# Two transformer layers on one core: the first weight group, GpSimd's copies, the first transpose and the last copies are arranged anew

## The chip, the core and the metric

The kernel runs on one core of a Trainium2 chip. The core has five engines, each with its own queue of instructions that it takes in order: TensorE (PE: matrix products, which write to PSUM), VectorE (DVE), ScalarE (ACT), GpSimd (POOL) and SyncE (SP, which here issues DMA transfers). Semaphores order the engines among each other. SBUF is the working memory, PSUM holds matmul results in 8 banks. The metric is the device time of one execution in microseconds; the profile is of a single execution of its own.

## The reference

```python
def _A_ref(x, wqkv, wo):                 # H = 32 heads of 16, S = 2048, D = 512
    qkv = (x @ wqkv).reshape(B, S, 3, H, Dh)...
    scores = einsum("bhqd,bhkd->bhqk", q, k) * Dh ** -0.5
    o = einsum("bhqk,bhkd->bhqd", softmax(scores), v)
    return o... @ wo
def _B_ref(x, w1, w2):                   # Dff = 1792
    return relu(x @ w1) @ w2
for both layers:
    x = x + _A_ref(layernorm(x), wqkv, wo)
    x = x + _B_ref(layernorm(x), w1, w2)
```

All inputs are bf16; both layers use the same weights.

## The kernel before, in words

**The stream of exps.** Each of the two layers has 32 heads x 2048 x 2048 scores. They are made in slots: in a slot TensorE writes three banks of 128 x 512 scores (`ps_s0` or `ps_s1`, in turn; line 1692), and ScalarE takes the exponential of them in one instruction (line 1705) into one of five buffers `e`. In most slots ScalarE takes only two banks (1024 columns); the third is read by VectorE, which makes an approximate exponential of three such banks by integer arithmetic (`lin`, line 1278; `up` and `down`, line 1330). The weighted sums with V go to `ps_o` (line 1158, "PV"): a round is up to four matmuls of 32 columns of weights side by side, one for each of four head pairs, and starts 0.216 us after the one before. K, Q and V projections, the output projection and the two feed-forward products are groups of such rounds (line 539) that fill TensorE's time between the scores; VectorE takes their results out of `ps_f` or `ps_o`.

**The plan.** What TensorE and VectorE do between the scores is decided while the program is built: a planner holds times of its own for TensorE (`now_pe`), VectorE (`now_dve`), the exps (`exp_end`), the SP queue (`sp_free`) and GpSimd (`pool_free`), and puts into each slot what it takes to be ready. `fill_v(limit, least)` places PV rounds if at least so many of the four head pairs have a block ready. When TensorE is too idle over the plan's window of 3.4 us, the same scores are written again (`times`). Constants tell the plan when x rows (`X_AT`), weight groups (`WQ_AT`) and V's weights (`WV_AT`) are there. `sp_lag` adds each issue on SP to `sp_free`. The engines run the resulting lists in order, with semaphores; a wait that the plan did not foresee blocks what stands behind it.

**The head.** x rows and weights are loaded by DMAs from SP, ScalarE and GpSimd queues. The columns of `wqkv` for K and Q are loaded in four groups T of 128 columns, K (k=0) and Q (k=1) each, and put in another order by one copy for each (`interleave`, line 205: `stage` to `wkq`). Group 0 of K is copied by ScalarE after its first two `xnT` copies, group 0 of Q by VectorE after the fourth normalized row; GpSimd copies the other three groups, as the DMAs land. Four rows of 128 tokens are normalized (statistics at line 575, root on GpSimd at line 1387, `head_apply` at line 1404), transposed on TensorE (line 635) and copied to `xnT` (line 1416; the first two by ScalarE, the last two by VectorE), with matmuls in between that only keep TensorE busy (line 1356). Then come the first K and Q projections (line 1422), Q's scaling (line 1455) and the first slot. Later chunks of 512 tokens are normalized by VectorE (line 626) and transposed by DMAs that SP issues (line 675).

**The tail.** After the last slot the last 128 rows are finished in line: output projection, normalization, transposition into one bank of `ps_o`, two half copies to `xnT` (line 1860: VectorE, then ScalarE), first feed-forward product in 14 steps with relu by VectorE and ScalarE in turn (lines 1885 and 1883), second product into one bank of 512 columns (line 1776), and two half copies of 256 columns out of that bank (line 1899: ScalarE, VectorE), each followed by its DMA to the output (line 1900).

Of the kernel before, what the change touches and what calls it, by code (L numbers as in the profile page):

```python
# [12 lines left out]
BF16 = mybir.dt.bfloat16  # L13
# [12 lines left out]
def kernel(  # L26
# [60 lines left out]
    BOTH = 4  # L87
    WHOLE = 4
    STARTS, MORE, ORDER = {}, {}, {}
    X_AT = (9.9, 10.1, 11.0, 11.4, 11.6, 11.9, 12.2, 12.5, 13.5, 14.5, 15.0, 15.5)  # L90
    WQ_AT, WV_AT = {0: 0.0, 1: 12500.0, 2: 16500.0, 3: 17900.0}, 9900.0
    VLAG = 1
    RSTD_LAG = 4000.0
    Q_SPARE = 6
# [21 lines left out]
    def sb(shape, dt, name):  # L116
        return persist.tile(shape, dt, name=name)
# [62 lines left out]
    ta2 = sb([P, 2, TPC], FP32, "ta")  # L180
    ta_ = [ta2[:, n] for n in range(2)]
    warm = sb([P, 1], FP32, "warm")

    ps_s = [psum.tile([P, W, QS], FP32, name=f"ps_s{n}") for n in range(2)]
    ps_o = psum.tile([P, QS], FP32, name="ps_o")
# [17 lines left out]
    def interleave(copy, k, T):  # L203

        copy(
            out=wkq[:, k, T].rearrange("p c (g d e) -> p (c g) e d", g=4, e=2),
            in_=stage[:, k, T].rearrange("p c (g e d) -> p (c g) e d", g=4, e=2),
        )
# [84 lines left out]
        made[key] = (engine, (now_pe if engine == "pe" else now_dve)[0] + lag)  # L293

    sp_free = [0.0]
    pool_free = [0.0]
    spread_till = [0.0]

# [350 lines left out]
    def ln_rows(tag, tt, n, i):  # L649

        if tag not in ln_seq:
            ln_seq.append(tag)
        at_tag = ln_seq.index(tag)
        prev = ln_seq[at_tag - 1]
        rows_of_prev = chunks[prev[1:]][1]
        before_that = ln_seq[at_tag - 2] if at_tag > 1 else None
        old = each(chunks[before_that[1:]][1], "xn", before_that) if at_tag > 1 else []
        if ("st", tag, i) not in made:
            loaded = [("x", tt + i)] * (tag[0] == "ln1" and not tag[1])
            task(720, lambda: ln_stats(tag, tt + i, i), [("st", tag, i)], old + loaded)  # L660
        if i == n - 1:

            def rstd():
                ln_seed(tag, n)
                pool_free[0] = max(pool_free[0], now_dve[0]) + RSTD_LAG
                mark(("rs", tag, 3), lag=pool_free[0] - now_dve[0])

            task(0, rstd, [("rs", tag, 3)], each(n, "st", tag) + old)
            def apply(k):
                ln_apply(tag, tt + k, k)  # L670
                if not by_dma(tag):
                    return
                _, l, j = tag
                xn_waits[0] -= k == TPC - 1
                nc.sync.dma_start_transpose(
                    out=xnT[j][:, :, k * P : (k + 1) * P], in_=xnbuf[k][:]
                )
                lag = sp_lag(TRANSPOSE) + (CROWDED if now_dve[0] < LOADED else 0.0)
                mark(("xT", tag, k), lag=lag)
                mark(("xnT", tag, k), lag=lag)  # L680
                if k == TPC - 1:
                    xn_free[0] = now_dve[0] + lag

            for k in range(n):
                task(
                    325, lambda k=k: apply(k),
                    [("xn", tag, k)] + [("xT", tag, k), ("xnT", tag, k)] * by_dma(tag),
                    [("xT", prev, k)] * (k < rows_of_prev) + [("rs", tag, 3)]
                    + [("raw",)] * (k == TPC - 1 and ("raw",) in made),
                )  # L690
# [700 lines left out]
        if not n:  # L1391
            set_ones(11, 16)
    for k in range(2):
        interleave(nc.gpsimd.tensor_copy, 1 - k, 1)
    set_ones(16, len(ones))
    for T in range(2, 4):
        for k in range(2):
            interleave(nc.gpsimd.tensor_copy, k, T)

    def head_bank(n, w):  # L1400
        return ps_s[n][:, w, :] if n < 2 else ps_f[:]

# [36 lines left out]
    for n in range(2):  # L1439
        for i in range(n * HALF, (n + 1) * HALF):  # L1440
            head_apply(i)
        if n:
            interleave(nc.vector.tensor_copy, 1, 0)
        for i in range(n * HALF, (n + 1) * HALF):
            head_transpose(i)
        if not n:
            interleave(nc.scalar.copy, 0, 0)
        idle_matmuls((4, 3)[n])
    head_k(0, P, (2, 0))
    for i in range(TPC):  # L1450
        head_q(i)
# [68 lines left out]
    pace = 0.0  # L1520
    recents = [[], []]
    readers = [[], []]
    now_pe[0] = 10900.0
    now_dve[0] = 12400.0
    exp_end = {-1: 10400.0, 0: 11400.0}
    pool_free[0] = WQ_AT[3]
    sp_free[0] = 15500.0
    pair_at = None
# [11 lines left out]
    while units:  # L1540
# [128 lines left out]
        for kind in ("v", "f", "v") if late else ("f", "v", "f"):  # L1669
            if kind == "f":  # L1670
                fill_pe(limit)
            else:
                fill_v(limit, 3 if len(pend) > 2 else 4)

        spare = int(max(need_by - pe_start("s", s_ready), 0.0) / MM)
        soon = (len(pend) > 1) + (owed[0] > 1.0 and (bool(cur) or not evac and any(
# [177 lines left out]
    while evac:  # L1854
        do_evac()
    for i in rows:
        pt = ln_transpose(tag, i, at_bank(more[i]).bitcast(BF16), more[i])
        for n, copy in enumerate((nc.vector.tensor_copy, nc.scalar.copy)):
            cs = slice(n * NDC // 2, (n + 1) * NDC // 2)
            uses(copy(out=xnT[NQS - 1][:, cs, part(i)], in_=pt[:, cs]), more[i], "xnT")  # L1860
    run_all()
    assert not w1_to_load
    ending[0], wide[0] = False, True
# [1 line left out]

    while half_done[0] < NF:
        half_part()
    for i in rows:
        add(banks[i], ident[:], x_t[tt + i][:], True, False, "x")
    for ft in range(NF + LOOK):  # L1870
        if ft == NF // 2:
            for b, x, row in outs:
                uses(nc.scalar.copy(out=x, in_=at_bank(b)), b)
                nc.sync.dma_start(out=out_flat[row * P : (row + 1) * P, :], in_=x)
        if ft < NF:
            b = more[ft % 4]
            for c in range(NDC):
                add(
                    b, w1_last[ft][:, c, :], xnT[NQS - 1][:, c, at_column : at_column + width],
                    c == 0, c == NDC - 1, "xnT",  # L1880
                )
            if ft % 2:
                out = nc.scalar.activation(out=ht[ft][:, at_column : at_column + width], in_=at_bank(b)[:, 0:width], func=ACTF.Relu)
            else:
                out = nc.vector.tensor_scalar(
                    out=ht[ft][:, at_column : at_column + width], in0=at_bank(b)[:, 0:width],
                    scalar1=0.0, scalar2=None, op0=ALU.max,
                )
            uses(out, b, "h")
        if ft >= LOOK:  # L1890
            for i in rows:
                add(
                    banks[i], ht[ft - LOOK][:, part(i)], w2[:, ft - LOOK, :],
                    False, ft == NF + LOOK - 1, "h",
                )
    for i in rows:
        for copy, queue, a in ((nc.scalar.copy, nc.scalar, 0), (nc.vector.tensor_copy, nc.sync, D // 2)):
            cols = slice(a, a + D // 2)
            uses(copy(out=x_t[tt + i][:, cols], in_=at_bank(banks[i])[:, cols]), banks[i])
            queue.dma_start(  # L1900
                out=out_flat[(tt + i) * P : (tt + i + 1) * P, cols], in_=x_t[tt + i][:, cols]
            )


# [28 lines left out]
```

## Time and profile before

| | |
|---|---|
| median of 3 runs | 1451.44 us (1450.73 to 1453.77) |
| the profiled execution | 1455.52 us; span of its instructions 1453.8 us |
| busy: ScalarE, TensorE, VectorE, GpSimd | 1424.2, 1366.6, 1312.1, 97.6 us |
| exps of 1536, 1024 and 512 columns | 369, 996 and 1 (1518, 1094 and 678 ns each) |
| first exp starts, last exp starts | 13.75 us, 1436.92 us |
| mean granted TensorE clock | 0.999 |

The span runs from the first to the last instruction of the profiled execution. Durations of successive exps overlap by some 0.19 us: starts of exps that are not held up lie 1.331 us apart behind one of 1536 columns and 0.904 us behind one of 1024. In lines of the timeline the first two numbers are start and length in microseconds; in brackets stands how long the engine was idle before, and what ended that. In lines of the windows each engine has its busy time and count, then come the granted TensorE clock, the DMA share and GB/s.

### The profile page before, as it was taken

Reading aid. Unit: us, or ns where it says so; the run is one execution under the profiler, and the core shown is the slowest. Engines: PE = TensorE matmul, PEld = TensorE weight load, DVE = VectorE, ACT = ScalarE, POOL = GpSimd, SP = SyncE. Lnnn points to the kernel's source line nnn. Section 1 sums busy time; section 2 is a strip of 40 time slices with the busy share of each in tenths; the row PEclk is TensorE's granted clock in tenths of the full one; section 3 lists DMA queues with packets and bytes.
Section 4 is the critical chain, followed back from the end, with each engine's and each line's share of the span. In section 5 each row is a group of like instructions: output and inputs, shape, how many; then the busy total and the mean of one; then the engine's idle time right before and its main releaser. Section 6 shows DMA issues by size and latency. Waiting matters only on the chain.

```text
span 1453.8 us, 47075 instructions
## 1 busy us (share of the span) xinstructions
PE 1366.6 (94%) x20730; PEld 507.1 (35%) x20732; DVE 1312.1 (90%) x2421; ACT 1424.2 (98%) x1385; POOL 97.6 (7%) x248
## 2 busy tenths in 40 slices
PE   8899999999999999999899999889999999999998
PEld 3222223222222222322323223222234444545665
DVE  7979999999999899999599889899989689999954
ACT  6999999999999999999999999999999999999996
POOL 5000001001010011000000000001001001010000
PEclk9999999999999999999999999999999999999999
DMA  5301100211012010110101000000110210313020
GB/s 142 84 6 25 23 11 16 44 27 31 10 26 48 19 22 10 39 42 17 24 5 37 24 5 2 10 15 13 44 41 20 50 36 23 74 35 80 13 59 19
DMA packets 135182, 46.23 MB, mean 32 GB/s; under 512 B 119968, under 2 KB 132192, under 8 KB 134976
## 3 DMA queue, kind: packets, MB, share of 16 engines
q1 hardware_dynamic: 127920, 37.08, 10.8%
q0 software_dynamic: 5568, 5.15, 1.9%
q8 instruction: 162, 2.65, 0.7%
q10 hardware_dynamic: 1488, 0.98, 0.2%
q14 instruction: 44, 0.36, 0.1%
HBM read 24.38 MB, written 2.10 MB: 18 GB/s over the span
## 4 chain that ended last, share of the span: by engine, by line
ACT 67%; PE 22%; DVE 9%; issue 1%; DMA 1%; POOL 0%; DVEq 0%; ACTq 0%
ACT e L1705 67%; PE ps_s L1692 7%; PE ps_f L539 7%; PE ps_o L1158 6%; DVE lin L1278 3%; DVE up L1330 1%; DVE down L1330 1%; PE ps_s L1776 1%; DVE ht L864 1%; PE ps_f L532 1%; DVE stats L575 0%; DVE q L787 0%; DVE vaug L771 0%; DVE x L904 0%; DVE ht L1025 0%
## 5 line engine op out<-in xcount | busy, mean ns | idle before, releaser
L1705 ACT ACTIVATE e<-ps_s 128x1024 bf16<-128x1024 f32 (+1 forms) x1366 | 1416.2, 1209 | 7.9 <-PE ps_s L1692 5.6
L1278 DVE TENSOR_SCALAR lin<-ps_s 128x512 int16<-128x512 f32 x996 | 664.1, 683 | 30.1 <-PE ps_s L1692 24.6
L1692 PE MATMUL ps_s<-q,ktp 32*128 32x512 bf16 (+2 forms) x6208 | 576.6, 324 | 48.3 <-ACT e L1705 42.7
L1158 PE MATMUL ps_o<-e,vaug 128*32 128x512 bf16 (+2 forms) x4318 | 395.8, 326 | 6.5 <-DVE r L1050 1.3
L1692 PEld LDWEIGHTS <-ktp 32*128 32x128 bf16 x6208 | 180.1, 91 | 520.3 <-issue 504.0
L1158 PEld LDWEIGHTS <-vaug 128*32 128x32 bf16 x7135 | 176.0, 95 | 225.9 <-issue 196.5
L1330 DVE TENSOR_SCALAR up<-lin 128x1536 int16<-128x1536 int16 x332 | 182.5, 550 | 12.0 <-PE ps_o L1158 11.2
L1330 DVE TENSOR_SCALAR down<-lin 128x1536 int16<-128x1536 int16 x332 | 182.0, 548 | 2.5 <-PE ps_o L1158 2.5
L1158 PE MATMUL ps_o<-up,vaug 128*32 128x512 bf16 (+2 forms) x1314 | 171.3, 329 | 0.0
L1158 PE MATMUL ps_o<-lin,vaug 128*32 128x512 bf16 (+2 forms) x1314 | 159.9, 329 | 1.3 <-DVE ht L1023 0.6
L1158 PE MATMUL ps_o<-down,vscaled 128*32 128x512 bf16 (+2 forms) x1125 | 148.7, 333 | 0.0
L539 PE MATMUL ps_f<-w,ht 128*32 128x512 bf16 x1680 | 130.7, 382 | 1.5 <-DVE ht L864 0.9
L539 PE MATMUL ps_f<-xnT,w 128*32 128x512 bf16 (+1 forms) x1792 | 123.7, 355 | 6.2 <-DVE ht L864 3.8
L539 PE MATMUL ps_f<-xnT,wkq 128*32 128x512 bf16 (+2 forms) x1376 | 102.5, 354 | 8.0 <-DMA xnT<-xn 2.3
L864 DVE TENSOR_SCALAR ht<-ps_f 128x512 bf16<-128x512 f32 (+1 forms) x111 | 74.2, 668 | 23.5 <-PE ps_f L539 16.6
L539 PEld LDWEIGHTS <-w 128*32 128x32 bf16 x1792 | 41.7, 95 | 43.0 <-issue 31.7
L1158 PEld LDWEIGHTS <-vscaled 128*32 128x32 bf16 x1125 | 49.7, 96 | 18.6 <-issue 10.6
L539 PEld LDWEIGHTS <-ht 128*32 128x32 bf16 x1680 | 35.9, 95 | 39.3 <-issue 27.0
L539 PEld LDWEIGHTS <-wkq 128*32 128x32 bf16 x1376 | 33.2, 95 | 39.1 <-issue 30.5
L539 PE MATMUL ps_f<-wv,xnT 128*32 128x512 bf16 x480 | 38.9, 387 | 6.9 <-DVE vaug L771 3.8
L575 DVE BATCH_NORM_STATS2 stats<-x 128x6 f32<-128x512 bf16 x63 | 42.3, 682 | 1.5 <-DMA x<-in_A_x_dram 1.2
L539 PE MATMUL ps_f<-wo,ot 128*32 128x512 bf16 x496 | 41.4, 382 | 0.7 <-DVE x L825 0.5
(138 smaller groups left out, 552.0 us busy)
## 6 DMA issues: line engine op xcount, KB each, us to landing
w<-in_B_w_dram SPq DMA_DIRECT2D x144, 128.0 KB
q<-xn SPq DMA_DIRECT2D x42, 64.0 KB
out_dram<-x SPq DMA_DIRECT2D x15, 128.0 KB
x<-in_A_x_dram SPq DMA_DIRECT2D x14, 128.0 KB
u<-r POOLq DMA_DIRECT2D x12, 128.0 KB, 4.7
ktp<-in_B_w_dram SPq DMA_DIRECT2D x10, 128.0 KB
u<-ht POOLq DMA_DIRECT2D x6, 128.0 KB, 4.4
r<-r SPq DMA_DIRECT2D x6, 128.0 KB
```

Source lines behind the costliest of these rows:

```text
L532: nc.tensor.matmul(out, lhsT, rhs, start=i % k == 0, stop=i % k == k - 1, skip_group_check=True,)
L539: nc.tensor.matmul(out[cols], lhsT[:, cols], rhs, start=i % k == 0, stop=i % k == k - 1, tile_position=(0, 32 * g), skip_group_check=True,)
L575: nc.vector.bn_stats(out=stats[ln_n(tag)][:, i, :], in_=x_t[tt][:])
L864: nc.vector.tensor_scalar(out=out, in0=sums, scalar1=0.0, scalar2=None, op0=ALU.max)
L1158: nc.tensor.matmul(ps_o[32 * g : 32 * g + 32, 0 : sg["w"]], values[:, 4 * sg["T"] + g, 2 * e : 2 * e + 32], rhs, start=g not in sg["begun" ...
L1278: first = nc.vector.tensor_scalar(out=lin[which][:, half * QS : (half + 1) * QS], in0=src, scalar1=EXP_BIAS, scalar2=0.0, op0=ALU.add, op1 ...
L1330: nc.vector.tensor_scalar(out=out, in0=line, scalar1=by, scalar2=0.0, op0=ALU.add, op1=ALU.max)
L1692: score = nc.tensor.matmul(b[:, a : a + sg["w"]], kt[32 * g : 32 * g + 32, kc : kc + P], qbuf[sg["n"] % 2][32 * g : 32 * g + 32, sg["e"], ...
L1705: ex = nc.scalar.activation(out=eb[:, 0 : place[m]], in_=b[:, 0 : place[m]], func=ACTF.Exp, scale=1.0 / (LOG2E * UNIT),)
L1776: uses(nc.tensor.matmul(out, lhsT, rhs, start=first, stop=last), b, needs=needs)
```

## The change

ScalarE makes both copies of group 0 (K and Q), before its two `xnT` copies; VectorE has no such copy any more. GpSimd first copies one column of the fourth normalized row into a new tile `after`, which makes it wait for that row, and then does its six weight copies and a dozen memsets, in the order T = 1, memsets, T = 2, T = 3. The plan counts 1.6 us more on SP behind the first DMA transpose, has other times for x, the weights and the start of the stream, and PV rounds are placed with three ready head pairs of four whatever is pending. In the tail the transposed last rows go into two banks, one for each half copy, and the last product into two banks of 256 columns, one for each of the last copies; the number of its matmuls doubles, with half the columns each.

```diff
--- before.py
+++ after.py
@@ -87,8 +87,9 @@
     BOTH = 4
     WHOLE = 4
     STARTS, MORE, ORDER = {}, {}, {}
-    X_AT = (9.9, 10.1, 11.0, 11.4, 11.6, 11.9, 12.2, 12.5, 13.5, 14.5, 15.0, 15.5)
-    WQ_AT, WV_AT = {0: 0.0, 1: 12500.0, 2: 16500.0, 3: 17900.0}, 9900.0
+    X_AT = (8.3, 8.5, 9.5, 10.6, 11.0, 11.4, 11.8, 12.1, 12.5, 12.8, 13.3, 14.0)
+    WQ_AT, WV_AT = {0: 0.0, 1: 10600.0, 2: 16000.0, 3: 17400.0}, 10200.0
+    FIRST_TRANSPOSE = 1600.0
     VLAG = 1
     RSTD_LAG = 4000.0
     Q_SPARE = 6
@@ -180,6 +181,7 @@
     ta2 = sb([P, 2, TPC], FP32, "ta")
     ta_ = [ta2[:, n] for n in range(2)]
     warm = sb([P, 1], FP32, "warm")
+    after = sb([P, 1], BF16, "after")
 
     ps_s = [psum.tile([P, W, QS], FP32, name=f"ps_s{n}") for n in range(2)]
     ps_o = psum.tile([P, QS], FP32, name="ps_o")
@@ -293,6 +295,7 @@
         made[key] = (engine, (now_pe if engine == "pe" else now_dve)[0] + lag)
 
     sp_free = [0.0]
+    first_transpose = [FIRST_TRANSPOSE]
     pool_free = [0.0]
     spread_till = [0.0]
 
@@ -675,6 +678,8 @@
                 nc.sync.dma_start_transpose(
                     out=xnT[j][:, :, k * P : (k + 1) * P], in_=xnbuf[k][:]
                 )
+                sp_free[0] = max(sp_free[0], now_dve[0] + 200.0) + first_transpose[0]
+                first_transpose[0] = 0.0
                 lag = sp_lag(TRANSPOSE) + (CROWDED if now_dve[0] < LOADED else 0.0)
                 mark(("xT", tag, k), lag=lag)
                 mark(("xnT", tag, k), lag=lag)
@@ -1391,12 +1396,7 @@
         if not n:
             set_ones(11, 16)
     for k in range(2):
-        interleave(nc.gpsimd.tensor_copy, 1 - k, 1)
-    set_ones(16, len(ones))
-    for T in range(2, 4):
-        for k in range(2):
-            interleave(nc.gpsimd.tensor_copy, k, T)
-
+        interleave(nc.scalar.copy, k, 0)
     def head_bank(n, w):
         return ps_s[n][:, w, :] if n < 2 else ps_f[:]
 
@@ -1439,13 +1439,15 @@
     for n in range(2):
         for i in range(n * HALF, (n + 1) * HALF):
             head_apply(i)
-        if n:
-            interleave(nc.vector.tensor_copy, 1, 0)
         for i in range(n * HALF, (n + 1) * HALF):
             head_transpose(i)
-        if not n:
-            interleave(nc.scalar.copy, 0, 0)
         idle_matmuls((4, 3)[n])
+    nc.gpsimd.tensor_copy(out=after[:], in_=xnbuf[TPC - 1][:, 0:1])
+    for T in range(1, 4):
+        for k in range(2):
+            interleave(nc.gpsimd.tensor_copy, k, T)
+        if T == 1:
+            set_ones(16, len(ones))
     head_k(0, P, (2, 0))
     for i in range(TPC):
         head_q(i)
@@ -1520,9 +1522,9 @@
     pace = 0.0
     recents = [[], []]
     readers = [[], []]
-    now_pe[0] = 10900.0
-    now_dve[0] = 12400.0
-    exp_end = {-1: 10400.0, 0: 11400.0}
+    now_pe[0] = 10950.0
+    now_dve[0] = 12500.0
+    exp_end = {-1: 10450.0, 0: 11450.0}
     pool_free[0] = WQ_AT[3]
     sp_free[0] = 15500.0
     pair_at = None
@@ -1670,7 +1672,7 @@
             if kind == "f":
                 fill_pe(limit)
             else:
-                fill_v(limit, 3 if len(pend) > 2 else 4)
+                fill_v(limit, 3)
 
         spare = int(max(need_by - pe_start("s", s_ready), 0.0) / MM)
         soon = (len(pend) > 1) + (owed[0] > 1.0 and (bool(cur) or not evac and any(
@@ -1854,10 +1856,17 @@
     while evac:
         do_evac()
     for i in rows:
-        pt = ln_transpose(tag, i, at_bank(more[i]).bitcast(BF16), more[i])
         for n, copy in enumerate((nc.vector.tensor_copy, nc.scalar.copy)):
-            cs = slice(n * NDC // 2, (n + 1) * NDC // 2)
-            uses(copy(out=xnT[NQS - 1][:, cs, part(i)], in_=pt[:, cs]), more[i], "xnT")
+            cs = range(n * NDC // 2, (n + 1) * NDC // 2)
+            pt = at_bank(more[n]).bitcast(BF16)
+            for c in cs:
+                uses(
+                    nc.tensor.transpose(
+                        pt[:, c * P : (c + 1) * P], xnbuf[i][:, c * P : (c + 1) * P], ident[:]
+                    ), more[n],
+                )
+            pt = pt[:, 0 : NDC * P].rearrange("p (c f) -> p c f", c=NDC)[:, cs.start : cs.stop]
+            uses(copy(out=xnT[NQS - 1][:, cs.start : cs.stop, part(i)], in_=pt), more[n], "xnT")
     run_all()
     assert not w1_to_load
     ending[0], wide[0] = False, True
@@ -1865,8 +1874,9 @@
 
     while half_done[0] < NF:
         half_part()
-    for i in rows:
-        add(banks[i], ident[:], x_t[tt + i][:], True, False, "x")
+    halves = [(banks[0], slice(0, D // 2)), (banks[1], slice(D // 2, D))]
+    for b, cols in halves:
+        add(b, ident[:], x_t[tt][:, cols], True, False, "x")
     for ft in range(NF + LOOK):
         if ft == NF // 2:
             for b, x, row in outs:
@@ -1888,18 +1898,16 @@
                 )
             uses(out, b, "h")
         if ft >= LOOK:
-            for i in rows:
+            for b, cols in halves:
                 add(
-                    banks[i], ht[ft - LOOK][:, part(i)], w2[:, ft - LOOK, :],
+                    b, ht[ft - LOOK][:, part(0)], w2[:, ft - LOOK, cols],
                     False, ft == NF + LOOK - 1, "h",
                 )
-    for i in rows:
-        for copy, queue, a in ((nc.scalar.copy, nc.scalar, 0), (nc.vector.tensor_copy, nc.sync, D // 2)):
-            cols = slice(a, a + D // 2)
-            uses(copy(out=x_t[tt + i][:, cols], in_=at_bank(banks[i])[:, cols]), banks[i])
-            queue.dma_start(
-                out=out_flat[(tt + i) * P : (tt + i + 1) * P, cols], in_=x_t[tt + i][:, cols]
-            )
+    for (b, cols), copy, queue in zip(
+        halves, (nc.scalar.copy, nc.vector.tensor_copy), (nc.scalar, nc.sync)
+    ):
+        uses(copy(out=x_t[tt][:, cols], in_=at_bank(b)[:, 0 : D // 2]), b)
+        queue.dma_start(out=out_flat[tt * P : (tt + 1) * P, cols], in_=x_t[tt][:, cols])
 
 
 # ---- launch: one core; inputs and outputs as the reference has them ----
```

## The prediction

> **What bounds the kernel now.** I read the page first, then the chain in order of time for the first 30 us, the timeline of the head, of 24 to 46 us and of the tail, and the windows around 31 us.
>
> ```profile
> ACT 67%; PE 22%; DVE 9%; issue 1%; DMA 1%; POOL 0%; DVEq 0%; ACTq 0%
> ...
> L1705 ACT ACTIVATE e<-ps_s 128x1024 bf16<-128x1024 f32 (+1 forms) x1366 | 1416.2, 1209 | 7.9 <-PE ps_s L1692 5.6
> ```
>
> ScalarE's exps are the spine: 1416.2 us busy, only 7.9 idle. The first starts at 13.75 and the last at 1436.92, so the time is head + exps + tail, and a gain must shorten an end, fill a hole in the exps, or leave them fewer elements.
>
> The chain of the head:
>
> ```profile
> 7.83 1.18 DVE xn L1404 x2
> 9.01 1.98 DVE wkq L205
> 10.99 0.31 DVE xnT L1416
> 11.30 0.04 issue
> 11.34 1.07 PE ps_s L1422 x16
> ```
>
> VectorE's copy of one weight piece is on the path for 1.98 us. The same copy takes ScalarE 0.79. The timeline shows why:
>
> ```profile
> 8.04 1.59 POOL L205 COPY wkq<-w 128x512 bf16<-128x512 bf16 x2 [0.24 <-DMA w<-in_A_wqkv_dram]
> 8.16 0.85 DVE L1404 TENSOR_SCALAR xn<-x,mv,half_ya 128x512 bf16<-128x512 bf16 x1
> 8.69 0.79 ACT L205 COPY wkq<-w 128x512 bf16<-128x512 bf16 x1
> 8.93 2.06 DVE L205 COPY wkq<-w 128x512 bf16<-128x512 bf16 x1
> ```
>
> While GpSimd copies, a VectorE instruction from SBUF to SBUF is stretched: the fourth normalization takes 0.85, the three before it 0.41.
>
> The largest hole in the exps (ScalarE's timeline, then the windows):
>
> ```profile
> 34.54 1.45 ACT L1705 ACTIVATE e<-ps_s 128x1536 bf16<-128x1536 f32 x1 [1.37 <-PE ps_s L1692]
> 36.91 2.60 ACT L1705 ACTIVATE e<-ps_s 128x1536 bf16<-128x1536 f32 x2 [0.92 <-PE ps_s L1692]
> ```
> ```profile
> 31.00:34.40 3.40, 1.06 (x14) 0.33 (x11) 1.89 (x5) 2.16 (x2) 2.26 (x6) 1.00 0.40 81
> 34.40:37.80 3.40, 3.40 (x34) 0.86 (x31) 0.69 (x1) 2.34 (x2) 0.00 (x0) 0.51 0.56 114
> ```
>
> TensorE stands 2.34 us at 31.4 to 33.8 until chunk 1's DMA transposes land (the first is issued in 2.74 us, later ones in 1.22). It is busy 1.06 us in that window, and then runs at half clock (0.51). Against the usual spacing of 1536-column exps, 1.331 us, those that follow the starts at 31.63, 34.54 and 36.91 are late by 1.57, 1.04 and 0.24: 2.86 us.
>
> **The change, part by part.**
>
> *Head.* VectorE loses its 2.06 copy. ScalarE gets both copies of group 0, ahead of its two xnT copies, and each waits for its DMA. In the trace's landing records the two pieces are in at 5.75 and 6.46; two copies of 0.79 end at about 7.25, and the first xnT copy has its transposes at 7.73. Cover 0.48; later landings cost what exceeds it. GpSimd now waits for the fourth normalized row; behind that wait stand six weight copies, twelve memsets and chunk 1's rstd chain. It ends at 8.16 + 0.41 = 8.57; the first two copies then run to about 10.5, and their weights are first used at 19.0. The other four still wait for DMAs that land from 13.66 on and ended at 15.83; the rstd chain (17.05 before, 15.75 wanted now) starts by 15.9, and its rows are normalized at 24.4, so nothing waits.
>
> Next on the path is TensorE's own order. Second-half transposes stay at 8.72, behind idle matmuls: 8 x 0.056, three idle matmuls x 0.216, four K matmuls x 0.056, so the Q matmuls start at 8.72 + 0.45 + 0.65 + 0.22 = 10.04 instead of 11.34: **-1.30**. They need the xnT copies, which VectorE starts at 9.13 and ends at 9.86 (0.40 each, 0.33 apart); the third Q block comes at 10.48, the fourth at 10.70.
>
> These copies run beside GpSimd's. The trace has no xnT copy beside one: bounds 0.40 (the q scaling, also from PSUM, took 0.73 beside GpSimd's copy at 13.78 and 0.75 alone) and 2.06 (the weight copy, SBUF to SBUF). The first is nearer in source; I take 0.40. The Trainium skill, "SBUF — State Buffer", Who interferes with whom, says the second of a VectorE copy in a two-port mode and a GpSimd instruction "fully blocks"; the 0.85 agrees. Its page "VectorE: DVE Perf Modes" keeps PSUM operands out of that mode; by it too the sum stays, and if the lock held here it would be the port rival below.
>
> *The first transpose in the plan.* The host-side plan adds 1.6 us behind the first transpose, so it places chunk 1's first K group behind the scores of exp 16, not 14, and repeats those scores four times to keep TensorE streaming. Up to exp 13 the order is the same, so all moves 1.30 earlier: transposes issued from 23.5, landed at 33.63 - 1.30 = 32.33, K group reached after exp 14's end (31.78), the switch and four score rounds: about 32.7. No wait: **-2.86**; the three extra rounds (0.65) end just when exp 16 is due: **+0.1**. In the worst 3.4 us there TensorE streams about half the time (0.216 us for each 512 columns, about 1.7 in all); the trace's lowest stretch without a lost clock is near that (0.53 at 65.1 to 68.5), the one that lost it 0.20. If the hole in other executions is smaller (that fourth landing straggled 1.04 us from first to last, the others 0.15 to 0.2), the gain may be only 0.6.
>
> The Trainium skill, "TensorE: Matmul & The Clock Gate", Why this matters, warns of idle gaps over about 3 us; here 2.34 sufficed, and the measurement decides. Its window is free-running, so executions may differ.
>
> *The stream.* Order lists give 372 exps of 1536 and 993 of 1024 columns, before 369 and 996. The rows by form are 1518 and 1094 ns: 3 x 0.424 = **+1.27**. The round rule (`fill_v` asks for 3 groups of four, never 4) and retimed loads reshuffle the rest. Counted: 1715 PV rounds against 1709, 1535 score rounds against 1523, projection work equal: 18 x 0.216 = 3.9 us of TensorE in 1366.6, mostly in its free time; VectorE loses three bank reads (0.68 each), three shifts (0.55 each) and three masked q writes (1.22 each) and gains three q copies of about 0.7: some 5 us less. After exp 25 the exps lose 27.9 us in all against their cadences (1.331, and 0.904 for 1024 columns). Worst are stretches where TensorE's rounds exceed ScalarE's ten exps: 1.69 us over at exps 655 and 851, which lost 1.8 and 2.6. The new order has 2.7 over at 653, 1.6 at 833. I take **0**, bounds -3 and +6.
>
> *Tail.* Halves of the last transposed row go to two banks, so ScalarE's copy need not wait for VectorE's: it starts at 1442.99 instead of 1443.31: **-0.32**. Last copies likewise: VectorE's (0.42) starts at TensorE's end, about 1450.12, not after ScalarE's at 1450.54: **-0.42**, and the last output DMA with it. The price: 256-column matmuls, 28 for 14. 128-column ones with their own weights go 0.056 apart, so 0.11 each: +0.03; were 14 weight loads of 0.10 laid bare, 1.4.
>
> *Sum:* -1.30 - 2.86 + 0.10 + 1.27 + 0 - 0.74 + 0.03 = **-3.5**. The profiled execution took 1455.52 (span 1453.8 and 1.7 around it): 1452.0. The median of the runs shown is 4.08 lower; the same step gives 1451.44 - 3.5 = **1447.9**.
>
> **The rivals.**
>
> *The hole is mostly the profiled execution's.* The straggling landing and 4.08 us over the median speak for it; the page can't refute it. Gain 3.5 - 2.3: 1450.2. Chance 0.17.
>
> *The reshuffled stream loses more (slower).* One mechanism: stretches in which TensorE's rounds exceed ScalarE's exps, first 653 to 663, where the scores come late. It decides once the loss after exp 25 passes 27.9 + 3.5 = 31.4 us; slower by over 0.2% from 34.3. At +7 the time is 1454.9. For it: 2.7 us over instead of 1.69, and 60% more than that over the whole run is not excluded. Against: equal total work. Chance 0.17.
>
> *The plan's delay does not remove the wait.* The slack is 0.4 us; transposes landing 1 us later, or an xn row late behind GpSimd, bring the wait back at exp 16 and perhaps the half clock: 2.0 lost, 1449.9. Chance 0.08.
>
> *The port.* xnT copies block until GpSimd's copies and memsets end, 10.5 + 1.14 = 11.6; Q starts near 11.8 and the head gains nothing: 1447.9 + 1.8 = 1449.7. The weight copy's 2.06 speaks for it, the q scaling against. Chance 0.04.
>
> The forecast keeps 0.54.
>
> **The numbers.** About 0.2%, 2.9 us, is what a measurement of this kernel can tell. The forecast lies 3.5 below, its own spread from the stream mostly 2: faster 0.45 of its 0.54, else same; some smaller part of the first and third rivals falls below 1448.5 where the stream gains (0.07). Faster 0.52; slower, 0.16, from the second rival; same 0.32. The range runs from a stream that gains 3.5 (1444.4) to half of the second rival (1452.6).
>
> **What would show it.** First exp near 12.45; ScalarE's weight copies over by 7.3; normalizations of 0.41; xnT copies of 0.40 beside GpSimd's; no wait on the transposes and clock 1.00 from 28 to 40 us; 16.9 - 0.7 from the last exp's start to the end. Wrong if the first exp comes after 13, if the clock falls near 33, or if exps after 25 lose over 31.

## The result, and the profile after

The changed kernel takes 1455.44 us (median of 11 runs, 1454.57 to 1456.95), the kernel before 1451.06 (11 runs, 1450.72 to 1453.77): a ratio of 1.0029, interval 1.0020 to 1.0038. It is slower by 4.4 us, where 3.5 less was forecast. The profiled execution took 1454.99, span 1453.1, which is an ordinary one. The profiled execution of before (1455.52) was not: it is longer than ten of its kernel's eleven runs by 4 us or more. That turns out to matter.

The page of after, the chain's share by engine and the group of the exps:

```profile
ACT 76%; PE 17%; DVE 5%; issue 1%; DMA 0%; DVEq 0%; ACTq 0%
...
L1707 ACT ACTIVATE e<-ps_s 128x1024 bf16<-128x1024 f32 (+1 forms) x1366 | 1418.0, 1207 | 7.9 <-PE ps_s L1694 5.4
```

ScalarE is as idle in front of the exps as before, 7.9 us, though the largest hole is gone: other idle time has come in its place.

The chain of the head, and its timeline:

```profile
9.17 0.65 PE ps_o L1361 x3
9.81 0.22 PE ps_f L1422 x4
10.04 0.91 PE ps_s L1422 x16
```
```profile
7.27 1.38 ACT L207 COPY wkq<-w 128x512 bf16<-128x512 bf16 x2 [4.14 <-DMA w<-in_A_wqkv_dram]
7.67 0.73 DVE L1404 TENSOR_SCALAR xn<-x,mv,half_ya 128x512 bf16<-128x512 bf16 x2 [0.27 <-POOL half_ya L1392]
8.61 0.76 POOL L207 COPY wkq<-w 128x512 bf16<-128x512 bf16 x1
8.98 0.76 DVE L1416 COPY xnT<-ps_s 128x512 bf16<-128x512 bf16 x2 [0.57 <-PE ps_s L638]
```

TensorE's own order (transposes, idle matmuls, K matmuls) now ends last, and the Q matmuls start at 10.04, to the hundredth as worked out. VectorE's two `xnT` copies (8.98 to 9.74) take 0.76 together, although GpSimd's copy runs beside them until 9.37. ScalarE's weight copies wait for their DMA until 7.27 and end at 8.65, not 7.3; its `xnT` copies end at 9.58, still ahead of the K matmuls at 9.81. The first exp starts at 12.29.

ScalarE's timeline behind the first DMA transposes, and the two windows there:

```profile
27.51 13.66 ACT L1707 ACTIVATE e<-ps_s 128x1536 bf16<-128x1536 f32 x11
```
```profile
31.00:34.40 3.40, 2.78 (x38) 0.97 (x36) 0.92 (x3) 3.40 (x4) 1.24 (x2) 1.00 0.43 87
34.40:37.80 3.40, 3.22 (x41) 1.02 (x36) 2.48 (x5) 3.40 (x4) 0.00 (x0) 1.00 0.35 72
```

Eleven exps without a gap where before had two starts late by a wait, TensorE busy for 2.78 of 3.40 us instead of 1.06, and the clock stays at 1.00.

The tail, from the timeline: the two copies to `xnT` and the two last copies.

```profile
1443.21 0.29 DVE L1869 COPY xnT<-ps_o 128x256 bf16<-128x256 bf16 x1 [0.38 <-PE ps_o L1864]
1443.32 0.37 ACT L1869 COPY xnT<-ps_s 128x256 bf16<-128x256 bf16 x1 [1.37 <-PE ps_s L1864]
...
1449.90 0.37 ACT L1909 CAST x<-ps_s 128x256 bf16<-128x256 f32 x1 [0.49 <-PE ps_s L1778]
1450.01 0.42 DVE L1909 CAST x<-ps_s 128x256 bf16<-128x256 f32 x1 [1.02 <-PE ps_s L1778]
```

Both pairs run side by side. From the start of the last exp to the end of the span it is 15.74 us; before 16.83.

What got longer is the middle. ScalarE's timeline near the end of the second layer:

```profile
1337.89 16.25 ACT L1707 ACTIVATE e<-ps_s 128x1024 bf16<-128x1024 f32 x14
1355.02 14.89 ACT L1707 ACTIVATE e<-ps_s 128x1024 bf16<-128x1024 f32 x14 [0.89 <-PE ps_s L1694]
1370.88 3.94 ACT L1707 ACTIVATE e<-ps_s 128x1024 bf16<-128x1024 f32 x4 [0.97 <-PE ps_s L1694]
```

And before, in the same exps:

```profile
1337.53 12.73 ACT L1705 ACTIVATE e<-ps_s 128x1024 bf16<-128x1024 f32 x12
1350.42 8.24 ACT L1705 ACTIVATE e<-ps_s 128x1536 bf16<-128x1536 f32 x7 [0.15 <-PE ps_s L1692]
1359.10 26.17 ACT L1705 ACTIVATE e<-ps_s 128x1024 bf16<-128x1024 f32 x24 [0.45 <-PE ps_s L1692]
```

After has two waits of 0.89 and 0.97 for the scores; the longest of before there is 0.45. From the first exp's start to the last's it is 1425.05 us, in before's profiled execution 1423.17, and in its ordinary ones, as the experiments show, 1419.9 to 1421.4.

### The profile page after: what moved, and what is told of

Same layout as the page of the kernel before. It is cut to its first block, busy times and chain, and to the rows that moved or that the text cites. A ratio compares the mean times of both kernels' runs of the same rounds, so it can differ in the third digit from the quotient of the medians.

```text
span 1453.1 us, 47371 instructions
## 1 busy us (share of the span) xinstructions
PE 1368.8 (94%) x20884; PEld 511.7 (35%) x20885; DVE 1307.2 (90%) x2414; ACT 1426.5 (98%) x1386; POOL 96.7 (7%) x249
## 3 DMA queue, kind: packets, MB, share of 16 engines
q8 instruction: 163, 2.67, 0.8%
## 4 chain that ended last, share of the span: by engine, by line
ACT 76%; PE 17%; DVE 5%; issue 1%; DMA 0%; DVEq 0%; ACTq 0%
ACT e L1707 76%; PE ps_s L1694 5%; PE ps_f L542 5%; PE ps_o L1163 5%; DVE lin L1283 2%; PE ps_s L1778 1%; DVE down L1335 1%; DVE up L1335 1%; DVE vaug L776 0%; DVE x L909 0%; DVE ht L869 0%; DVE stats L578 0%; DMA x<-in_A_x_dram 0%; DVE u L1055 0%; PE ps_o L542 0%
## 5 line engine op out<-in xcount | busy, mean ns | idle before, releaser
L1163 PE MATMUL ps_o<-e,vaug 128*32 128x512 bf16 (+2 forms) x4318 | 389.4, 326 | 8.1 <-DVE r L1055 3.5
L1694 PEld LDWEIGHTS <-ktp 32*128 32x128 bf16 x6346 | 183.5, 91 | 523.4 <-issue 507.0
L1163 PE MATMUL ps_o<-down,vscaled 128*32 128x512 bf16 (+2 forms) x1107 | 152.3, 335 | 0.0
L542 PE MATMUL ps_f<-w,ht 128*32 128x512 bf16 x1680 | 135.0, 382 | 0.9 <-DVE x L909 0.7
L542 PEld LDWEIGHTS <-w 128*32 128x32 bf16 x1792 | 41.3, 95 | 39.6 <-issue 28.6
L587 POOL TENSOR_TENSOR ta<-stats 128x4 f32<-128x4 f32 (+2 forms) x17 | 4.8, 281 | 604.0 <-DVE stats L578 604.0
```

The lines of the kernel that those rows point to most:

```text
L542: nc.tensor.matmul(out[cols], lhsT[:, cols], rhs, start=i % k == 0, stop=i % k == k - 1, tile_position=(0, 32 * g), skip_group_check=True,)
L587: pool.tensor_tensor(out=t1, in0=st[:, :, 1], in1=st[:, :, 4], op=ALU.subtract)
L1163: nc.tensor.matmul(ps_o[32 * g : 32 * g + 32, 0 : sg["w"]], values[:, 4 * sg["T"] + g, 2 * e : 2 * e + 32], rhs, start=g not in sg["begun" ...
L1694: score = nc.tensor.matmul(b[:, a : a + sg["w"]], kt[32 * g : 32 * g + 32, kc : kc + P], qbuf[sg["n"] % 2][32 * g : 32 * g + 32, sg["e"], ...
```

## The experiments

In all of them "loss" is the prediction's measure: the start of the next exp less the cadence (1.331 us after a 1536-column exp, 0.904 after one of 1024), summed. Exps are counted from 1. The table is worked out from the exps of each profiled execution. e10 stands for an ordinary execution of before: it has before's list of instructions on every engine, but for a few matmuls that stand in another order or are missing in the trace.

| | time | first exp | loss, exps 14–16 | loss after exp 25 | of it 640–670 | of it 1285–1320 | last exp to end |
|---|---|---|---|---|---|---|---|
| before | 1455.52 | 13.75 | 2.86 | 27.9 | 1.94 | 1.48 | 16.83 |
| e10 (before's list) | 1451.03 | 12.27 | 0.19 | 27.5 | 1.94 | 1.07 | 16.84 |
| after | 1454.99 | 12.29 | 0.02 | 31.4 | 3.30 | 3.38 | 15.74 |
| e1 head and tail | 1450.56 | 12.37 | 0.52 | 27.3 | 1.94 | 1.09 | 16.07 |
| e2 plan | 1455.66 | 12.18 | 0.02 | 31.2 | 3.30 | 3.36 | 16.73 |
| e3 all but the round rule | 1453.88 | 12.43 | 0.03 | 28.6 | 2.67 | 2.14 | 15.98 |
| e4 ends and round rule | 1452.95 | 12.46 | 0.00 | 30.5 | 3.30 | 2.87 | 15.97 |
| e12 first transpose | 1453.70 | 12.18 | 0.03 | 28.1 | 2.67 | 1.48 | 16.73 |
| e13 rule, no repeats | 1450.34 | 12.04 | 0.27 | 28.4 | 3.31 | 1.28 | 16.73 |

**First split: ends, plan, round rule.** Four kernels of one batch, measured together; before took 1451.00 (27 runs) beside them.

*e1* is before with the new head and the new tail; the plan (constants, first transpose, round rule) is the old one.

```diff
--- after
+++ e1
-    FIRST_TRANSPOSE = 1600.0
...
-                sp_free[0] = max(sp_free[0], now_dve[0] + 200.0) + first_transpose[0]
-                first_transpose[0] = 0.0
...
-    now_pe[0] = 10950.0
+    now_pe[0] = 10900.0
...
-                fill_v(limit, 3)
+                fill_v(limit, 3 if len(pend) > 2 else 4)
```

> The kernel before with the new head and the new tail, and the old plan: the order of the exps and of all between them is that of before. Theory A (the two ends gain what the profile after shows, 1.46 and 1.1 us, and the new plan's order of the stream costs about 7): 1451.1 - 2.5 = 1448.5, ratio 0.9983. Theory B (the ends gain nothing in the whole, because the stream gives back what the head saves): 1451, ratio 1.000. Theory C (the new head or tail itself costs the 4.4 us): 1455, ratio 1.003.

Measured 1450.60 (1449.88 to 1450.93), ratio 0.9994 (0.9985 to 1.0003). The two ends lose nothing, and what they gain can't be told from none.

*e2* is the reverse: the old head and tail with the whole new plan.

```diff
--- before
+++ e2
+    FIRST_TRANSPOSE = 1600.0
...
+                sp_free[0] = max(sp_free[0], now_dve[0] + 200.0) + first_transpose[0]
...
-                fill_v(limit, 3 if len(pend) > 2 else 4)
+                fill_v(limit, 3)
```

> The old head and the old tail with the whole new plan (times of x and weights, the first transpose, the start, PV rounds of three). Theory A: 1455.4 + 2.5 = 1457.9, ratio 1.0047. Theory B: 1455.4, ratio 1.003. Theory C: 1451, ratio 1.000.

Measured 1455.66 (5 runs), ratio 1.0035 (1.0023 to 1.0048). All of the loss is in the plan. The number is theory B's, but not for its reason: the stream gives nothing back, the old head starts the exps just as early here (12.18).

*e3* is after with the old round rule.

```diff
--- after
+++ e3
-                fill_v(limit, 3)
+                fill_v(limit, 3 if len(pend) > 2 else 4)
```

> The changed kernel with the old rule for PV rounds (three ready of four only where more than two slots are pending). If the rule is what costs the stream: 1448 to 1449, ratio 0.998 to 0.9985. If the new times of the plan cost it: about 1455, ratio 1.003. If any new order costs some 3 to 7 us against the one before: 1451 to 1455.

Measured 1453.10 (1452.68 to 1453.88), ratio 1.0013 (1.0004 to 1.0022). Its list has 375 wide exps where before has 369, 6 x 0.427 = 2.6 us; the loss after exp 25 is 28.6, as against 31.4 with the rule.

*e4* is e1 with the new rule alone.

```diff
--- e1
+++ e4
-                fill_v(limit, 3 if len(pend) > 2 else 4)
+                fill_v(limit, 3)
```

> New head, new tail and the new rule for PV rounds, with the old times in the plan and no delay behind the first transpose. If the rule costs the stream: about 1455, ratio 1.003. If the new times cost it: 1448.5, ratio 0.998. If any new order costs some 3 to 7 us: 1451 to 1455.

Measured 1453.68 (1452.78 to 1456.19), ratio 1.0019 (1.0011 to 1.0028): 3.1 us over e1 with as many exps of each width, and 30.5 - 27.3 = 3.2 us more loss after exp 25. The rule alone costs this. From about exp 160 on, e4's list is the same as after's: the new times and the delay behind the first transpose change only what is ahead of that, where after has three more wide exps and 0.4 us more loss.

**Where the head's gain went.** Before took 1451.26 (27 runs) in this batch.

*e5* is before, unchanged, once more.

> The kernel before, unchanged, in another profiled execution. Theory D (the head's 1.46 us and most of the hole behind the first transposes belonged to the one execution that was profiled: GpSimd's weight piece landed at 7.98, so that its copy met VectorE's): the piece lands near 10, VectorE's weight copy takes about 0.45, the first exp starts at 12.2 to 12.4, the hole at exp 14 costs about 0.5, the span is 1449 to 1449.5. Rival (the old head is always that slow, and the old tail or plan made up for it in the plan-only kernel): first exp at 13.7, weight copy 2.06.

It took 1452.35, a single run. The timeline of its head:

```profile
8.37 0.46 DVE L205 COPY wkq<-w 128x512 bf16<-128x512 bf16 x1
...
10.02 1.42 POOL L205 COPY wkq<-w 128x512 bf16<-128x512 bf16 x2 [2.34 <-DMA w<-in_A_wqkv_dram]
...
12.33 1.45 ACT L1705 ACTIVATE e<-ps_s 128x1536 bf16<-128x1536 f32 x1 [0.19 <-PE ps_s L1692]
```

With the old head, VectorE's weight copy takes 0.46, not 2.06, and GpSimd waits for its own weight piece until 10.02; in the first profile of before that piece was there at 8.04. Q matmuls start at 10.08 and the first exp at 12.33, as in after. The conflict that the new head removes belonged to one execution: in the other profiles with the old head, but for e6 below, the copy takes 0.45 to 0.47.

*e6* forces it: GpSimd copies four x rows into a tile that is not yet in use, ahead of its weight copies.

```diff
--- before
+++ e6
+    for n in range(TPC):
+        nc.gpsimd.tensor_copy(out=ot[0][:], in_=x_t[n][:])
```

> The kernel before with four more GpSimd copies of 128x512 (x rows that are there, into a tile that is written again later) ahead of its weight copies, so that GpSimd copies while VectorE copies its weight piece in every execution. Theory D: that copy takes 2 us or more, first exp 13.3 to 13.8, time 1451.0 + 1.3 = 1452.3 (1451.5 if the stream takes some of it back). If the two engines do not block each other: copy 0.45, first exp 12.3, 1451.0.

Measured 1451.41, ratio 1.0000 (0.9991 to 1.0009). Its timeline:

```profile
7.78 2.95 POOL L1394 COPY ot<-x 128x512 bf16<-128x512 bf16 x4
7.85 1.35 DVE L1406 TENSOR_SCALAR xn<-x,mv,half_ya 128x512 bf16<-128x512 bf16 x2 [0.27 <-POOL half_ya L1387]
...
9.13 0.46 DVE L205 COPY wkq<-w 128x512 bf16<-128x512 bf16 x1
```

A normalization is stretched again (1.35 for two, 0.73 without), but the weight copy takes 0.46 in the midst of GpSimd's copies. So a copy beside GpSimd's is not always held up: the 2.06 is seen in one execution, and what brought it about stays open. These copies of GpSimd are not the ones of before, which put a weight piece in another order, and before's long copy outlasted those too: they ended at 9.63, GpSimd's memsets at 10.67, the copy at 10.99. The first exp came at 12.78, 0.4 later than usual; the span is 0.3 over e10's (1449.5 and 1449.2), less than the medians can tell. Exps 14 to 16 lost 0.08. That a later start gives the transposes slack is not shown: before started later still and lost 2.86 there.

*e7* and *e8* have the new tail alone and the new head alone.

```diff
--- before
+++ e7
-        pt = ln_transpose(tag, i, at_bank(more[i]).bitcast(BF16), more[i])
+            pt = at_bank(more[n]).bitcast(BF16)
...
+    halves = [(banks[0], slice(0, D // 2)), (banks[1], slice(D // 2, D))]
--- before
+++ e8
+        interleave(nc.scalar.copy, k, 0)
...
+    nc.gpsimd.tensor_copy(out=after[:], in_=xnbuf[TPC - 1][:, 0:1])
```

> The kernel before with the new tail alone: last transposes and last copies over two banks. The tail's sum says -0.7 to -1.1: 1450.1, ratio 0.9994. If doubling the matmuls costs what the banks save: 1451.0, ratio 1.000.

> The kernel before with the new head alone. Theory D: no gain in an ordinary execution, 1451.0 to 1451.2, ratio 1.000. By the prediction's step (head -1.3): 1449.7, ratio 0.999.

e7 took 1450.67, ratio 1.0000 (0.9991 to 1.0009); last exp to end 16.07. e8 took 1451.71, ratio 1.0001 (0.9992 to 1.0010): the new head brings nothing that can be measured. The profiled execution of e8 (1454.02) is one with the hole and the clock drop, and shows that these come and go with the execution, not with the head:

```profile
31.00:34.40 3.40, 2.18 (x26) 0.67 (x26) 0.90 (x2) 2.06 (x2) 1.06 (x2) 0.85 0.44 90
34.40:37.80 3.40, 3.40 (x33) 0.74 (x30) 1.16 (x3) 2.48 (x4) 0.00 (x0) 0.64 0.32 64
```

The same windows of e5, whose TensorE stood idle there just as long (2.30 us from one matmul to the next; 2.31 in e8, 2.34 in before):

```profile
31.00:34.40 3.40, 2.02 (x26) 0.75 (x27) 1.03 (x3) 2.07 (x2) 1.15 (x2) 1.00 0.41 84
34.40:37.80 3.40, 3.22 (x45) 1.05 (x44) 2.12 (x5) 3.40 (x5) 0.00 (x0) 1.00 0.37 75
```

**Is it the rule, or any reordering?** Before took 1451.49 (33 runs) in this batch. Three kernels change one group of the plan's numbers (e11 has the new `X_AT` as well), the fourth has the first transpose alone.

```diff
--- before
+++ e9
-    DVE_TO_DVE, EVAC = 112.0, 612.0
+    DVE_TO_DVE, EVAC = 113.0, 612.0
--- before
+++ e10
-    now_pe[0] = 10900.0
-    now_dve[0] = 12400.0
-    exp_end = {-1: 10400.0, 0: 11400.0}
+    now_pe[0] = 10950.0
+    now_dve[0] = 12500.0
+    exp_end = {-1: 10450.0, 0: 11450.0}
--- before
+++ e11
-    WQ_AT, WV_AT = {0: 0.0, 1: 12500.0, 2: 16500.0, 3: 17900.0}, 9900.0
+    WQ_AT, WV_AT = {0: 0.0, 1: 10600.0, 2: 16000.0, 3: 17400.0}, 10200.0
...
--- before
+++ e12
+    FIRST_TRANSPOSE = 1600.0
...
+                sp_free[0] = max(sp_free[0], now_dve[0] + 200.0) + first_transpose[0]
```

> Before, with one number of the plan off by 1 ns: its step from one VectorE instruction to the next, DVE_TO_DVE, is 113 for 112. Nothing in it is better or worse by intent; the list comes out in another order with the same widths (369 and 996 exps). Theory 'any reordering costs' (the old order is a picked one): stream loss after exp 25 of 29 to 32 us against 27.4, time 1452.7 to 1455. Theory 'the round rule costs' (only what asks for PV rounds with three head pairs loads the stretches at exps 650 to 665 and 1285 to 1320): loss 27.4, the two places 1.9 and 1.1, time 1451.2.

> Before, with only the three start times of the plan's stream from the change (now_pe 10950, now_dve 12500, exp_end 10450 and 11450); widths 369 and 996. 'Any reordering costs': loss after exp 25 of 29 to 32, time 1452.7 to 1455. 'The round rule costs': loss 27.4, time 1451.2.

> Before, with only the changed times for x rows and weights (X_AT, WQ_AT, WV_AT); widths 369 and 996. 'Any reordering costs': loss after exp 25 of 29 to 32, time 1452.7 to 1455. 'The round rule costs': loss 27.4, time 1451.2. If these times and not the order as such spoil it: this one near 1453, the other two at 1451.2.

> Before, with only the 1.6 us behind the first transpose in the plan; widths 375 and 990, which is 6 x 0.427 = 2.56 us more by the cadences. If the wait behind the transposes is gone as in every kernel with this line (exps 14 to 16 lose 0.0 instead of 0.1 to 2.9, mostly 0.5 to 1.6) and nothing else moves: 1451.2 + 2.6 - 1.0 = 1452.8. 'Any reordering costs' adds 1 to 4 us of loss after exp 25: 1454 to 1457. If the delay is worth what the prediction gave it (2.9): 1450.9.

e9 took 1451.75, e10 1451.64, e11 1451.55, ratios 1.0001, 1.0003 and 1.0000 (each 0.0009 either way). They do not test what they were made for: with the numbers of e10 and e11 TensorE's list is the same as before's, and e9 differs in a few rounds near the end. What e10 and e11 show is that the plan's new times cost and bring nothing by themselves. e12 tests it for a part of the run. Its list is another from exp 14 to exp 885 and before's again behind that, and it took 1453.70, ratio 1.0014 (1.0005 to 1.0023): 2.2 us, between its first two expectations. Its span is 2.8 over e10's (1451.9 and 1449.2): 2.56 for six wider exps, 0.55 more loss after exp 25, 0.16 less at exps 14 to 16, 0.20 less at the two ends. So this other order costs 0.55 us of loss, where the rule's costs 3 to 4 (e2, e4, after); one such order does not show what any order costs. At exps 640 to 670 it does lose more, 2.67 against 1.94. At exps 1285 to 1320 it can't be compared, since it has before's list there.

**What makes the rule's order late.** Two places hold nearly all of the additional loss of after: exps 640 to 670 (3.30 against 1.94) and 1285 to 1320 (3.38 against 1.07), together 3.7 of 31.4 - 27.5 = 3.9 us; what is gained and lost elsewhere nearly cancels. At the second place thirteen executions with before's list lose 1.06 to 2.14 (e3 the most), the three with the list of after 2.87 to 3.38 (after, e2, e4).

The first is work that the new order put there. The matmuls into `ps_f` (projections, feed-forward) from the start of exp 652 to that of exp 665, after and then e7, which has before's plan:

```profile
674.80:690.10 15.30, 8.35 (x104) 1.37 (x2) 0.00 (x0) 1.00 0.10 19
```
```profile
674.30:687.70 13.40, 6.50 (x88) 0.68 (x1) 0.00 (x0) 1.00 0.12 23
```

1.85 us more of them, in a stretch in which TensorE is busy for 14.58 of 15.30 us (13.07 of 13.40 in e7); the loss in these exps is 3.08 and 1.65. The rule is not alone in this: e12, with the old rule, has 7.71 us of them there and loses 2.49. That this work is the cause here is read from the traces and not tested, since no run takes it away again.

At the second place the plan, thinking TensorE idle, writes the same scores again: 468 score matmuls from the start of exp 1285 to that of exp 1311 in after, 324 in e7. *e13* is the new rule with the new tail, and no repeated scores in those slots; *e14* has the rule from slot 1250 on only; *e15* is e7 again. Before took 1451.14 (27 runs).

```diff
--- e7
+++ e13
-                fill_v(limit, 3 if len(pend) > 2 else 4)
+                fill_v(limit, 3)
...
-        times = 1 + min(spare, max(0, math.ceil(short / MM)))
+        times = 1 + min(spare, max(0, math.ceil(short / MM))) * (not 1284 <= no <= 1312)
--- e7
+++ e14
-                fill_v(limit, 3 if len(pend) > 2 else 4)
+                fill_v(limit, 3 if len(pend) > 2 or no > 1250 else 4)
```

> Before, with the new tail, the new round rule, and no repeated scores in slots 1284 to 1312 (in e4 there are 13 there). Widths 366 and 999: 1.28 us less than e4 by the cadences. Theory 'the repeats make the scores late': exps 1285 to 1320 lose 1.1 to 1.4 instead of 3.0, loss after exp 25 near 29.0, time 1453.5 - 1.3 - 1.7 = 1450.5. Theory 'PV rounds moved there and their waits': the loss there stays 2.5 to 3.3, time 1452.2.

> Before, with the new tail, and the new round rule from slot 1250 on only; widths 369 and 996. If the loss at exps 1285 to 1320 comes of the rule there: 2.9 to 3.3 lost, time 1450.7 + 1.8 = 1452.5. If it comes of what the rule reshuffled over the run before: 1.1 to 1.5 lost there, time 1450.7. Exps 640 to 670 lose 1.94 in both.

> Before, with the new tail only, once more. Tail gain as the trace showed it (0.78 from the last exp's start to the end): 1450.6, ratio 0.9995. If the gain were the profiled execution's only: 1451.3, ratio 1.0.

ScalarE's timeline there, e4 (the rule, with repeats) and e13 (without):

```profile
1337.23 15.56 ACT L1703 ACTIVATE e<-ps_s 128x1024 bf16<-128x1024 f32 x13
1353.67 1.02 ACT L1703 ACTIVATE e<-ps_s 128x1024 bf16<-128x1024 f32 x1 [0.89 <-PE ps_s L1690]
1354.97 13.73 ACT L1703 ACTIVATE e<-ps_s 128x1024 bf16<-128x1024 f32 x13 [0.27 <-PE ps_s L1690]
1369.12 2.86 ACT L1703 ACTIVATE e<-ps_s 128x1024 bf16<-128x1024 f32 x3 [0.43 <-PE ps_s L1690]
```
```profile
1337.37 35.70 ACT L1705 ACTIVATE e<-ps_s 128x1024 bf16<-128x1024 f32 x33
```

33 exps without a wait that the timeline shows. The loss at 1285 to 1320 is 1.28 instead of 2.87, the first place keeps its 3.31, and the clock is 1.00 here without the repeats too. The list of e13 is that of e4 up to exp 1288, and its widths up to exp 1297; over exps 1285 to 1297 e13 loses 0.49, e4 1.94, before 0.47. So the repeats are the cause at this place, together with what the plan orders otherwise once they are gone. From first exp to last e13 takes 1419.71 us, e4 1422.74: 1.28 of the 3.03 are three narrower exps that come with the edit, 1.75 are loss. The medians differ by less, 2.25 (1451.43, 1450.34 to 1454.33, against 1453.68), and the time lies between the two expectations. e13's tail is 16.73, 0.76 longer than e4's; from its last normalization to its last copy it takes 8.01 us for 7.60 (in after). Why, no run tells.

How e4's wait at 1353 comes about, from TensorE's timeline:

```profile
1346.59 1.09 PE L1690 MATMUL ps_s<-q,ktp 32*128 32x128 bf16 x48
...
1352.45 0.63 PE L1159 MATMUL ps_o<-e,vaug 128*32 128x128 bf16 x32 [0.39 <-DVE r L1051]
```

The 48 score matmuls are one set of twelve and three repeats of it, 0.27 us each here. From 1345.57 to 1352.06 TensorE has next to no idle time in which to catch up. Then a PV round has to wait until VectorE has read `ps_o` (`r`, 0.30 us), and the scores behind it come too late for the exp.

e14 took 1450.69, ratio 0.9998 (0.9989 to 1.0006), loss at 1285 to 1320 1.07. But its list is e7's up to exp 1334: behind before's order the rule decides nothing else in this stretch. So the loss there needs what the rule has moved earlier in the run; which of those moves, no run tells. e15 took 1450.67, ratio 0.9995 (0.9986 to 1.0004).

Of all kernels run, e1 (1450.60), e7 and e15 (both 1450.67) and e14 are the lowest. They beat the changed kernel by 4.8 us; each is 0.4 to 0.6 us under the before of its batch, which is inside the intervals.

## Why the prediction was wrong, by its steps

**The level.** The sum was made against the profiled execution and then carried to the median ("the same step gives 1451.44 - 3.5"), although that execution was 4.08 over it. This is the step that failed first. Against e10, with the same instructions and 4.5 us shorter, the excess is: first exp 13.75 - 12.27 = 1.48, exps 14 to 16 2.86 - 0.19 = 2.67, all else 0.4. The two largest terms of the sum, head and hole, were the profiled execution's excess; the median did not hold them, so they could not be taken off it.

Between the sum of -3.5 and the +3.9 worked out below lie 7.4 us: 3.9 of this level, 3.9 of the stream, and 0.4 that the tail gave back.

**Head, -1.30.** The mechanism was right and the new chain is to the hundredth (Q matmuls at 10.04), but in ordinary executions the old head has Q at the same time (10.08 in e5). Worth 0 within what the medians can tell: e8, ratio 1.0001. That the new chain came out has some luck in it: ScalarE's weight copies ended at 8.65 instead of 7.25, past the cover of 0.48 that the step gave them, and this cost nothing only because its `xnT` copies still ended 0.23 ahead of the K matmuls.

**Hole, -2.86.** The plan's delay removes the wait, every time: exps 14 to 16 lose 0.02 or 0.03 in after, e2, e3 and e12. But of the eleven executions that have the old order there (before, e1, e5 to e11, e14, e15), seven lose 0.00 to 0.52 and four 1.57 to 2.86 (before, e5, e8, e15), 0.95 in the mean. The rival that named this had 0.17; it was true, and true of the head as well, which it did not say.

**Widths, +1.27.** As counted: 372 and 993.

**Stream, 0, bounds -3 and +6.** Measured 31.4 - 27.5 = +3.9. This is the term that was mis-sized. The prediction named the place and the sign: it had 2.7 us too much for TensorE at exps 653 to 663 against 1.69, and the traces lost 3.08 (after) and 1.65 (e7) in exps 652 to 664. It then took 0 because total work was equal. Equal totals did not help: in this stretch, where TensorE is nearly full, 1.85 us more of matmuls came with 1.43 us more loss, and what other stretches were spared did not bring that back. The 12 additional score rounds, which the prediction counted as "mostly in its free time", stand at the second place and were not free there: the loss is 2.3 us more, and e13 shows most of it gone without them.

**Tail, -0.71.** 16.83 or 16.84 became 15.74 in after, 15.97 to 16.12 in e1, e3, e4, e7, e14 and e15: -0.7 to -1.1. From the start of the last normalization to the start of the last copy it is 7.60 us in after, 8.45 before.

With what the runs showed the sum against e10 is +0.02 (first exp) + 1.28 (widths) - 0.17 (hole) + 3.87 (stream) - 1.10 (tail) = +3.9, and the spans are 1453.1 and 1449.2.

**The slower rival** asked for a loss after exp 25 over 31.4 to end above before, and 34.3 to be slower by 0.2%. The loss was 31.4, and the kernel is slower by 0.3%, since these marks stood on gains of 4 us at head and hole that ordinary executions don't have. Its mechanism, scores that come late where TensorE has too much to do, is the one that decided; that repeated scores would bring on the larger part, far behind the place that it named, it did not say. The port rival and that of a delay that leaves the wait both fell: 0.76 for both `xnT` copies (in e5 too, where GpSimd stands idle beside them), and no wait.

## What to carry to other kernels

A profiled execution that is longer than the median holds something that the median does not: find first what it is, by a second profile of the same kernel, and do not price a gain on it. A planner's rule that moves work all along a kernel is to be costed at the places where the engine that supplies the bounding one is already full, not by totals. An edit to an end of a kernel and an edit to its plan belong in separate kernels; here the tail gained 0.7 to 1.1 us in the traces, and the plan hid it.

## What the runs showed of the hardware

The same idle time of TensorE can cost the clock or not. Four executions have a gap of 2.30 to 2.37 us from one matmul to the next near 30 to 32 us: before (0.51 in the next window), e8 (0.85 and 0.64), e5 and e15 (1.00). The two with a drop took 1454.0 and 1455.5, those with the gap alone 1451.5 and 1452.4; at exps 14 to 16 they lost 2.70 and 2.86, and 1.65 and 1.57. What differs among them is not the gap's length but where it falls. In the traces' clock records each change lies a whole number of 3.41 us behind the first grant of the full clock (at 7.13 us in before, 6.11 in e8, 4.29 in e5, 3.97 in e15), and the stretch at half clock near 34 us lasts 3.41. Windows cut at these steps, before and then e5:

```profile
31.02:34.43 3.41, 1.07 (x18) 0.34 (x15) 1.87 (x5) 2.14 (x2) 2.26 (x6) 1.00 0.40 82
34.43:37.85 3.42, 3.42 (x34) 0.85 (x31) 0.69 (x1) 2.39 (x2) 0.00 (x0) 0.50 0.56 113
```
```profile
28.18:31.60 3.42, 1.83 (x27) 0.62 (x27) 2.79 (x6) 3.42 (x3) 2.31 (x9) 1.00 0.39 79
31.60:35.01 3.41, 2.45 (x34) 0.99 (x38) 1.10 (x2) 2.08 (x3) 0.55 (x1) 1.00 0.57 115
```

In before and e8 all or nearly all of the gap lies in one step, in which TensorE is busy for 1.07 and 1.19 us, and the next step has half the clock. In e5 and e15 it is shared by two steps, busy for 1.83 and 2.45, 2.14 and 2.06, and the clock stays. Where between 1.19 and 1.83 the limit lies is not measured. The Trainium skill, "TensorE: Matmul & The Clock Gate", Part 1, What's actually happening, says that the activity window is free-running and does not start with the kernel. These four agree with that.

Behind the same eight DMA transposes, issued over 12.2 us in each, TensorE stood 2.3 us in those four and 0.62 to 1.25 in the other seven executions with the old order there (e1, e6, e7, e9, e10, e11, e14); what decides it is not shown.

GpSimd's first copy of a weight piece started at 8.04 in one execution of the old head; in ten others (e2, e5, e7, e9 to e15) it starts at 9.64 to 10.81, held by that piece's DMA each time, and GpSimd's copies do not meet VectorE's.
